# Two attention layers with their gradients on one core: sums of p k v^T over three blocks taken into the first pass, and their K blocks left out of the last

## The chip, the cores and the metric

One core of a Trainium2 chip. A time is the device time of one execution in microseconds (us); the time before is the median of three runs. PE is TensorE's matrix multiply, PEld its weight load, DVE VectorE, ACT ScalarE, POOL GpSimd, SP SyncE, which issues most loads. The arena is a part of SBUF; PSUM is where matmuls put their results.

## The reference

A decode step of four layers with its whole gradient: attention, feed-forward, attention, feed-forward, each after a layer norm and added to x. Both attention layers use the same K and V caches (4 key-value heads, called groups, of 65536 positions and 128 columns, 64 MiB each for K and V in bf16) and the same weights; 8 query heads share a group.

```python
def _A_ref(x, k_cache, v_cache, wq, wo):
    ...
    scores = jnp.einsum("bhqd,bhkd->bhqk", q, k) * (Dh ** -0.5)
    p = _softmax(scores, axis=-1)
    o = jnp.einsum("bhqk,bhkd->bhqd", p, v)
    ...
_out, _vjp = jax.vjp(_f, A_x, A_k_cache, A_v_cache, A_wq, A_wo, B_w1, B_b1, B_w2, B_b2)
_grads = _vjp(grad_out)
```

The outputs are x and the gradients of x, K, V and all weights and biases. The gradient of the query of a layer is, for each head, dq = scale x sum over positions of p (dO v^T - delta) k. Written out, that is dO applied to the 128 x 128 matrix sum of p k v^T, less delta times the vector sum of p k; so a part of the positions can be summed as matrix and vector in a pass in which dO is not yet known, and dq of these positions follows later without K and V.

## The kernel before

Each of the two layers needs p of all positions twice, forward and backward, and K and V do not fit on the chip. So they are read in four passes, p = 0 to 3 in the code (pass 1 to 4 in this text):

- **Pass 1** (`attn_fwd(0, L1, ...)`): forward of layer 1. K is turned by PE (`kT`, L1050) and copied out of PSUM by DVE or ACT (`evac`, L164 and L167), multiplied with the queries (`kS`, L1068), the exponentials are kept for all later passes in a plane of the arena per group (`E`), and V is multiplied with them (`v8`, L1151).
- **Pass 2** (`attn_fwd(1, L3, ...)`): the same for layer 3.
- **Pass 3** (`attn_bwd3(2, L3, ...)`): dq of layer 3: V is turned, multiplied with dO (`vS`), and K with the result (`k8`, L1379).
- **Pass 4** (`attn_bwd4`): dq of layer 1 and the gradients of K and V for both layers, which are stored. K is needed for dq of layer 1 alone (`k8`, L1570); V is turned (L1458) and multiplied with dO of both layers (`vS`, L1495). The outer products of the weights' gradients run in between.

Between the passes lie the dense parts: the last `wo`, the feed-forward layers, and the way back.

**Blocks, units, order.** A block is 4096 positions of one group (32 on each of 128 partitions), 1 MB for K and as much for V; a group has 16 blocks. A step of a pass handles 8 of the 32, so 4 steps make a block and 256 a pass. A unit is 4 blocks (16 steps); the running maximum of the softmax is renewed per unit. `ITEMS[p]` lists the steps of pass p. Before, passes 1 and 2 go group by group (0 to 3 up, then 3 to 0 down), so that the last K blocks of pass 1 stay in the arena for pass 2 (`plan_keep`, 8 K blocks; 7 V blocks each at the next two ends). `pipeline` runs the stages of a step with fixed lags, in that written order on PE, DVE and ACT (`manual_schedule`); pass 4 is not under it, and there the scheduler orders the instructions.

**The arena.** 20 slots of 1 MB: 12, and 8 that become the planes of exponentials of the two layers as the passes reach their groups (`plane`, `hold`). All else, loads of K, V and weights (`slabs`) and outputs, goes through the free slots; SP issues loads in program order, each as soon as its slot is free. In pass 1 two neighbouring free slots are taken at once where they are to be had (`NOW["pairs"]`, `take_pair`, L373: loads of 2 MB); the other passes load 1 MB at a time (L368).

**The sums of pass 2.** Three blocks (`SUMMED`), one of group 3 and two of group 2, are handled in pass 2 by `g_pkv` beside the pipeline: POOL makes the products p k (L1186, 4 heads at a time), PE multiplies V with them (L1179) and sums p k (L1195), one step of the generator per step of the pass, some 66 steps for a block. The results are kept in `PKV`, M (128 x 8 x 128) and S (128 x 8) per group, rescaled by DVE when the maximum has changed. K and V of such a block stay in the arena for as long (`KV["long"]`). Pass 3 then skips K and V of these blocks; `pkv_dq` (L1304, L1305) gives their part of dq from M, S, dO and delta (`nd2`), one call per group within pass 3, and `k8` adds it to the unit's sum.

**Background.** `Background` gives out other work by steps: `by_group` starts the generator of the next group's q (`g_q`) or dO some steps ahead of the group, and `need` runs what is left of it when the group begins. `dO_finish` (L971 to L985) ends each dO: dO itself, the delta product on PE (L976), and its two bf16 halves in `nd2`.

Of the kernel before, what the change touches and what calls it, by code (L numbers as in the profile page):

```python
# [20 lines left out]
def kernel(  # L21
# [251 lines left out]
    HELD, BUSY, RING = set(), set(), set()  # L273
    NOW = {"step": 0, "pairs": True, "wide": False, "newest": False, "ring": False}

# [3 lines left out]
    def plane(lay, g):  # L279

        return NSLOT + G + g if lay else NSLOT + G - 1 - g

# [71 lines left out]
    def kv8(t, g, c8):  # L354
# [3 lines left out]
        if key not in have:  # L358
            i = None
            if NOW["pairs"] and hb % 2 == 0 and (t, g, hb + 1) not in have and key not in KV["halves"]:  # L360
                i = take_pair()
            if i is None:
                at = None
                if key in KV["long"]:
                    at = min((f, i) for i, f in FREE.items() if i < NSLOT)[1]
                    del FREE[at]
                sl = Slot("blk_" + t, at=at, load=True)
                nc.sync.dma_start(out=sl.t.rearrange("p (j d) -> p j d", d=DH), in_=half(KVIN[t], g, hb))  # L368
                have[key] = sl
            else:  # L370
                for h in range(2):
                    have[(t, g, hb + h)] = Slot("blk_" + t, at=i + h)
                nc.sync.dma_start(out=wide(i).rearrange("p (j d) -> p j d", d=DH), in_=KVIN[t][g][hb // 2])  # L373
        return have[key].t.rearrange("p (j d) -> p j d", d=DH)[:, j:j + 8, :]

    def turned_to(t, g, c8, kb8):

        if KV["turn"] == t and (t, g, c8 // J) in KV["keep"] and (t, g, c8 // J) not in MKEYS:
            state_key = (t, g, c8)
# [53 lines left out]
    def start_pass(p):  # L433
# [363 lines left out]
    class Background:  # L797
# [36 lines left out]
        def by_group(self, p, gen):  # L834
# [188 lines left out]
    def attn_fwd(p, L, on_group, bg, end=()):  # L1023
# [116 lines left out]
        def v8(g, c8):  # L1140
# [18 lines left out]
        def g_pkv(g, hb):  # L1159

            ks, vs = (KV["have"][(t, g, hb)] for t in "kv")
            k3, v3 = (sl.t.rearrange("p (j d) -> p j d", d=DH) for sl in (ks, vs))
            M, S = PKV[g]
            before = next((b * J // SU for a, b in SUMMED if a == g and b != hb), None) if (g, hb) != next(m for m in SUMMED if m[0] == g) else None
            if before is None:
# [85 lines left out]
        last_unit = (items[-1][0], items[-1][1] // SU)  # L1251
        n = len(items) // G
        order = list(dict.fromkeys(g for g, _ in items))
        holds = [(k * n + 2, plane(p, g)) for k, g in enumerate(order) if k > 0]
# [25 lines left out]


    def attn_bwd3(p, L, on_group, bg, end=()):
        st = ExitStack()
# [8 lines left out]
        for g, c8 in items:  # L1292
# [3 lines left out]
            hblast[(g, c8 // HB)] = c8  # L1296

        def pkv_dq(g):

            M, S = PKV[g]  # L1300

            pt = ps_mv([P, 2, R])
            for h in range(R):
                nc.tensor.matmul(pt[:, 0, h:h + 1], lhsT=M[:, h, :], rhs=L["dOT"][:, g * R + h:g * R + h + 1], start=True, stop=True)  # L1304
            nc.tensor.matmul(pt[:, 1, :], lhsT=sel2[:, :], rhs=L["nd2"][:, gsl(g)], start=True, stop=True)  # L1305
            t = dspool.tile([P, R], F32, name="pkv_t", tag="pkv_t", bufs=1)
            nc.vector.tensor_tensor(out=t[:], in0=pt[:, 1, :], in1=S[:], op=ALU.mult)
            y = dspool.tile([P, R], F32, name="pkv_y", tag="pkv_y", bufs=1)
            nc.vector.tensor_tensor(out=y[:], in0=pt[:, 0, :], in1=t[:], op=ALU.add)
            state["pkv"] = y  # L1310

# [54 lines left out]
        def k8(g, c8):  # L1366
# [3 lines left out]
            if c8 == sufirst[(g, su)]:  # L1370
                state["ps_dq"] = ps_acc([P, 8, R])
                if SUM_AT.get(g) == su:
                    pkv_dq(g)
            ps_dq = state["ps_dq"]
# [8 lines left out]
            if c8 == sulast[(g, su)]:  # L1383

                def fold():
                    col = ps_dq[:, 0, :]
                    if SUM_AT.get(g) == su:
                        both = dspool.tile([P, R], F32, name="pkv_t", tag="pkv_t", bufs=1)
# [13 lines left out]
    def attn_bwd4(p, La, Lb, on_group, bg, stack, end=()):  # L1402
# [7 lines left out]
        glast = {g: [c8 for gg, c8 in items if gg == g][-1] for g in range(G)}  # L1410
        sufirst, sulast = {}, {}
        for g, c8 in items:
            sufirst.setdefault((g, c8 // SU), c8)
            sulast[(g, c8 // SU)] = c8

# [141 lines left out]

        def k8(g, c8):
            kb8 = kv8("k", g, c8)
            b, j0 = divmod(c8, J)  # L1560
            su = c8 // SU
            X = state[("X", g, b)]
            if c8 == sufirst[(g, su)]:
                state["ps_dq"] = ps_acc([P, 4, R2])
            ps_dq = state["ps_dq"]
            for i in range(8):
# [238 lines left out]
    PKV = {}
    pkv_stack = ExitStack()
    pkv_pool = pkv_stack.enter_context(tc.tile_pool(name="pkv", bufs=1))
    for g in SUM_AT:
        PKV[g] = pkv_pool.tile([P, R, P], F32, name="pkv_m%d" % g), pkv_pool.tile([P, R], F32, name="pkv_s%d" % g)
    attn_fwd(1, L3, on2, bg, [(3, pre_load("wo3", lambda: wo_slabs(lastg[1], 2)))])  # L1810
# [261 lines left out]
    with tc.manual_schedule(engines=ORDERED):  # L2072
# [125 lines left out]
```

## Time and profile before

| | us |
|---|---|
| median of three runs | 1920.0 |
| the three runs | 1920.0, 1918.35, 1925.62 |
| the profiled execution | 1925.24 |
| its span | 1923.5 |

| engine | busy us | share of the span |
|---|---|---|
| PE | 1618.7 | 84% |
| PEld | 1301.0 | 68% |
| DVE | 1194.1 | 62% |
| ACT | 1046.0 | 54% |
| POOL | 340.0 | 18% |

DMA moves 781.38 MB at a mean of 406 GB/s. Of the loads, 60 are of 2048 KB (K 32, V 28, all in pass 1) and 364 of K and V of 1024 KB.

Rows of the profile: a group of instructions has line, engine, operation, out<-in with shapes, x count, then busy us and mean ns of one, then the idle time just before them and what ended it. In the table by stage a row is a window in us from the span's start, with each engine's busy us and instructions, the granted TensorE clock as a share of full speed, the share of time that the DMA engines are busy, and GB/s. In rows of waits, "SPq" is SP's DMA queue: what it waited for, us in total, times, longest.

### The profile page before, as it was taken

Reading aid. Unit: us, or ns where it says so; the run is one execution under the profiler, and the core shown is the slowest. Engines: PE = TensorE matmul, PEld = TensorE weight load, DVE = VectorE, ACT = ScalarE, POOL = GpSimd, SP = SyncE. Lnnn points to the kernel's source line nnn. Section 1 sums busy time; section 2 is a strip of 40 time slices with the busy share of each in tenths; the row PEclk is TensorE's granted clock in tenths of the full one; section 3 lists DMA queues with packets and bytes.
Section 4 is the critical chain, followed back from the end, with each engine's and each line's share of the span. In section 5 each row is a group of like instructions: output and inputs, shape, how many; then the busy total and the mean of one; then the engine's idle time right before and its main releaser. Section 6 shows DMA issues by size and latency. Waiting matters only on the chain. (4 is left out here: it accounts for less than half of the span.)

```text
span 1923.5 us, 67347 instructions
## 1 busy us (share of the span) xinstructions
PE 1618.7 (84%) x30165; PEld 1301.0 (68%) x30165; DVE 1194.1 (62%) x2471; ACT 1046.0 (54%) x1623; POOL 340.0 (18%) x517
## 2 busy tenths in 40 slices
PE   6878788689998987987888888889988979798896
PEld 6878777578887877887777775555555555455463
DVE  5645455266665664555464487767867777567685
ACT  3435343354443445455364376666867777567676
POOL 0000000005776760000000002111111112111121
PEclk9989998899999999999899999888988889789897
DMA  9999999999999999999999997999999999999997
GB/s 393 427 427 424 428 428 416 404 418 422 422 422 418 423 424 333 398 424 422 425 422 423 381 352 300 426 420 396 424 424 423 418 394 413 384 367 424 415 420 327
DMA packets 121489, 781.38 MB, mean 406 GB/s; under 512 B 11104, under 2 KB 18286, under 8 KB 43886
## 3 DMA queue, kind: packets, MB, share of 16 engines
q1 hardware_dynamic: 92894, 602.98, 76.0%
q0 software_dynamic: 24080, 165.70, 20.7%
q10 hardware_dynamic: 4224, 8.39, 1.1%
q8 instruction: 236, 3.87, 0.7%
q14 instruction: 55, 0.45, 0.1%
HBM read 611.33 MB, written 165.69 MB: 404 GB/s over the span
## 5 line engine op out<-in xcount | busy, mean ns | idle before, releaser
L167 DVE COPY kt<-ps_tr 128x1024 bf16<-128x1024 bf16 x728 | 498.9, 687 | 386.3 <-PE ps_tr L1050 217.1
L164 ACT CAST arena<-ps_gg 128x1024 bf16<-128x1024 f32 x457 | 444.4, 1011 | 200.4 <-PE ps_gg L1539 140.8
L1050 PE MATMUL ps_tr<-ident_b,arena 128*128 128x128 bf16 x3840 | 302.1, 222 | 27.6 <-DMA arena<-in_A_k_cache_dram 20.1
L164 ACT COPY kt<-ps_tr 128x1024 bf16<-128x1024 bf16 (+1 forms) x176 | 183.8, 1048 | 194.4 <-PE ps_tr L1320 105.6
L1050 PEld LDWEIGHTS <-arena 128*128 128x128 bf16 x3840 | 238.8, 99 | 55.3 <-DMA arena<-in_A_k_cache_dram 23.2
L167 DVE CAST arena<-ps_gg 128x1024 bf16<-128x1024 f32 (+2 forms) x186 | 222.2, 1195 | 85.1 <-PE ps_gg L1539 48.7
L1151 PE MATMUL ps_acc<-arena 128*128 128x64 bf16 (+4 forms) x4096 | 200.6, 195 | 45.7 <-DMA arena<-in_A_v_cache_dram 36.9
L1539 PE MATMUL ps_gg<-GG,xt 64*128 64x512 bf16 x1024 | 217.2, 421 | 16.5 <-ACT arena L164 5.4
L1186 POOL TENSOR_TENSOR pk<-arena 128x512 bf16<-128x512 bf16 x192 | 195.6, 1042 | 110.7 <-PE ps_m L1179 80.8
L1458 PE MATMUL ps_tr<-ident_b,arena 128*128 128x128 bf16 x1824 | 182.3, 236 | 37.5 <-DVE kt L167 19.3
L1068 PE MATMUL ps_sc<-L_qpad,kt 128*128 128x64 bf16 (+3 forms) x3648 | 183.1, 192 | 16.7 <-issue 8.1
L1133 ACT ACTIVATE arena<-S_sb,L_negm 128x128 bf16<-128x128 f32 x256 | 165.6, 1006 | 53.8 <-DVE L_negm L1118 45.5
L1151 PEld LDWEIGHTS <-arena 128*128 128x128 bf16 x4096 | 156.1, 100 | 50.6 <-DMA arena<-in_A_v_cache_dram 42.3
L1458 PEld LDWEIGHTS <-arena 128*128 128x128 bf16 x1824 | 121.2, 105 | 96.4 <-issue 76.0
L1320 PE MATMUL ps_tr<-ident_b,arena 128*128 128x128 bf16 x1904 | 150.8, 223 | 20.8 <-DMA arena<-in_A_v_cache_dram 19.1
L1068 PEld LDWEIGHTS <-kt 128*128 128x128 bf16 x3648 | 151.8, 99 | 22.3 <-issue 10.5
L661 POOL MEMSET rows_m<- 128x28 f32 (+1 forms) x3 | 0.4, 121 | 818.4 <-DVE rows_ym L754 818.4
L1545 POOL DMA_DIRECT2D out_dram<-arena x128 | 68.5, 535 | 409.6 <-ACT arena L164 263.9
L1570 PEld LDWEIGHTS <-arena 128*128 128x128 bf16 x2048 | 91.6, 102 | 60.7 <-issue 30.9
L1320 PEld LDWEIGHTS <-arena 128*128 128x128 bf16 x1904 | 114.1, 100 | 25.1 <-DMA arena<-in_A_v_cache_dram 21.4
L1133 ACT ACTIVATION_READ_ACCUMULATOR arena<-S_sb,L_negm 128x1 f32 x256 | 128.3, 501 | 0.0
L1495 PEld LDWEIGHTS <-kt 128*128 128x128 bf16 x1824 | 85.8, 102 | 50.4 <-issue 48.8
(359 smaller groups left out, 2475.6 us busy)
## 6 DMA issues: line engine op xcount, KB each, us to landing
arena<-in_A_v_cache_dram SPq DMA_DIRECT2D x183, 1024.0 KB, 16.4
arena<-in_A_k_cache_dram SPq DMA_DIRECT2D x181, 1024.0 KB, 16.7
out_dram<-arena POOLq DMA_DIRECT2D x149, 1024.0 KB, 15.3
arena<-in_A_k_cache_dram SPq DMA_DIRECT2D x32, 2048.0 KB, 28.5
arena<-in_A_v_cache_dram SPq DMA_DIRECT2D x28, 2048.0 KB, 29.9
arena<-in_A_wo_dram SPq DMA_DIRECT2D x30, 1024.0 KB, 17.0
arena<-in_B_w_dram SPq DMA_DIRECT2D x21, 1024.0 KB, 11.1
arena<-in_A_wq_dram SPq DMA_DIRECT2D x20, 1024.0 KB, 13.7
```

The lines of the kernel that those rows point to most:

```text
L164: nc.scalar.copy(out=out, in_=in_)
L167: nc.vector.tensor_copy(out=out, in_=in_)
L1050: nc.tensor.transpose(pt[:, i, :], kb8[:, i, :], ident_b[:, :])
L1068: nc.tensor.matmul(state["ps_s"][:, s:s + w, :].rearrange("p a b -> p (a b)"), lhsT=kt[:, i, :], rhs=L["qpad"][:, g, 0:w, :].rearrange("p ...
L1133: nc.scalar.activation(out=E(p, g, c0, SU)[:, :, h], in_=S[:, h, :], func=ACTF.Exp, bias=L["negm"][:, g, su, h:h + 1], scale=SCALE, accum_ ...
L1151: NOW["ps_o"] = nc.tensor.matmul(ps_o[:, 0:w, :], lhsT=vb8[:, i, :], rhs=E(p, g, c, w), start=(c % SU == 0), stop=(c % SU == SU - 1), skip ...
L1186: nc.gpsimd.tensor_tensor(out=r[:, :, :], in0=k3[:, j, :].unsqueeze(1).to_broadcast([P, 4, P]), in1=e4.unsqueeze(2).to_broadcast([P, 4, P] ...
L1320: nc.tensor.transpose(pt[:, i, :], vb8[:, i, :], ident_b[:, :])
L1458: nc.tensor.transpose(pt[:, i, :], vb8[:, i, :], ident_b[:, :])
L1495: nc.tensor.matmul(state["ps_dp"][:, s:s + w, :].rearrange("p a b -> p (a b)"), lhsT=vt[:, i, :], rhs=DOB[:, g, 0:w, :].rearrange("p a b - ...
L1539: nc.tensor.matmul(pg[:, 512 * h:512 * h + 512], lhsT=xt[64 * h:64 * h + 64, j1 // 8 + m, :], rhs=gg[64 * h:64 * h + 64, :, :].rearrange(" ...
L1570: nc.tensor.matmul(ps_dq[:, 0:w, :].rearrange("p a b -> p (a b)"), lhsT=kb8[:, i, :], rhs=X[:, s:s + w, :].rearrange("p a b -> p (a b)"), ...
```

## The change

- Pass 1 now also runs `g_pkv`, over blocks 0, 4 and 7 of group 3, for layer 1. M and S are opened ahead of pass 1 and closed ahead of pass 4.
- `pkv_dq` is called for layer 1 at the end of the dense part between pass 3 and pass 4, after dO of group 3; `k8` of pass 4 skips the three K blocks (their V is still loaded) and adds the result in unit 1 of group 3.
- The blocks summed in pass 2 are now blocks 8, 7 and 0 of group 3, all in one M and S; pass 3 skips three K and V pairs as before.
- The units of passes 1 and 2 come in an order written out: group 3's come between those of others. The planes, the holds and the starts of `by_group` follow that order.
- Loads of two slots at once are off in pass 1 (`NOW["pairs"]`).

```diff
-    NOW = {"step": 0, "pairs": True, "wide": False, "newest": False, "ring": False}
+    NOW = {"step": 0, "pairs": False, "wide": False, "newest": False, "ring": False}
...
-        return NSLOT + G + g if lay else NSLOT + G - 1 - g
+        return NSLOT + G + g if lay else NSLOT + G - 1 - list(dict.fromkeys(g for g, _ in ITEMS[0])).index(g)
...
-    ITEMS = [order_by_unit(False, SU), order_by_unit(True, SU), order_by_unit(False, HB), order_by_unit(True, J)]
+    def units(p, order):
+        assert sorted(order) == [(g, u) for g in range(G) for u in range(NSU)]
+        return [(g, c8) for g, u in order for c8 in range(u * SU, (u + 1) * SU, 8)]
+
+    ORDER1 = [(0, 0), (3, 0), (0, 1), (0, 2), (0, 3), (3, 1), (1, 0), (1, 1), (1, 2), (1, 3), (2, 0), (2, 1), (2, 2), (2, 3), (3, 2), (3, 3)]
+    ORDER2 = [(3, 3), (3, 2), (3, 1), (2, 3), (2, 2), (2, 1), (2, 0), (1, 3), (1, 2), (3, 0), (1, 1), (1, 0), (0, 3), (0, 2), (0, 1), (0, 0)]
+    ITEMS = [units(0, ORDER1), units(1, ORDER2), order_by_unit(False, HB), order_by_unit(True, J)]
     MG, MB = ITEMS[1][0][0], ITEMS[1][0][1] // J - 4
-    SUMMED = [(MG, MB), (MG - 1, MB), (MG - 1, 3)]
-    SUM_AT = {g: hb * J // SU for g, hb in SUMMED}
-    ITEMS[2] = [(g, c8) for g, c8 in ITEMS[2] if (g, c8 // J) not in SUMMED]
-    MKEYS = [(t,) + m for m in SUMMED for t in "kv"]
+    SUMS = [[(MG, 0), (MG, 4), (MG, 7)], [(MG, MB), (MG, 7), (MG, 0)]]
+    SUM_AT = [s[-1][1] * J // SU for s in SUMS]
+    ITEMS[2] = [(g, c8) for g, c8 in ITEMS[2] if (g, c8 // J) not in SUMS[1]]
+    MKEYS = [[(t,) + m for m in s for t in "kv"] for s in SUMS]
...
-        NOW["pairs"] = p == 0
+        NOW["pairs"] = False
         KV["halves"] = set(TOUCH[p][-8:])
-        KV["long"] = set(MKEYS if p == 1 else [])
+        KV["long"] = set(MKEYS[p] if p < 2 else [])
...
-                self.later.append((k * n + 8 if PS["pass4"] and k else k * n + n // (2 if p in (1, 2) and k == 0 else 4), gen(g), g))
+                first = next(i for i, (gg, _) in enumerate(ITEMS[p]) if gg == g) if p < 2 else (k + 1) * n
+                self.later.append((max(4, first - (n - 8 if PS["pass4"] and k else n // 2 if p in (1, 2) and k == 0 else 3 * n // 4)), gen(g), g))
...
-            if p == 1 and c8 % J == 0 and (g, c8 // J) in SUMMED:
+            if c8 % J == 0 and (g, c8 // J) in SUMS[p]:
                 sides.append(g_pkv(g, c8 // J))
...
-        PS["m"] = p == 1
+        PS["m"] = True
...
+    def pkv_dq(lay, L, pool):
+
+        M, S = PKV[lay]
+        pt = ps_mv([P, 2, R])
+        for h in range(R):
+            nc.tensor.matmul(pt[:, 0, h:h + 1], lhsT=M[:, h, :], rhs=L["dOT"][:, MG * R + h:MG * R + h + 1], start=True, stop=True)
+        nc.tensor.matmul(pt[:, 1, :], lhsT=sel2[:, :], rhs=L["nd2"][:, gsl(MG)], start=True, stop=True)
+        t = pool.tile([P, R], F32, name="pkv_t", tag="pkv_t", bufs=1)
+        nc.vector.tensor_tensor(out=t[:], in0=pt[:, 1, :], in1=S[:], op=ALU.mult)
+        y = vec.tile([P, R], F32, name="pkv_y%d" % lay)
+        nc.vector.tensor_tensor(out=y[:], in0=pt[:, 0, :], in1=t[:], op=ALU.add)
+        return y
...
         def k8(g, c8):
+            if (g, c8) == items[len(items) // G - 1]:
+                first_at(1, lambda: state["Xs"].free())
+            if (g, c8 // J) in SUMS[0]:
+                return
             kb8 = kv8("k", g, c8)
...
-                fold_dq(La, g, su, ps_dq[:, 0, 0:R], gfirst[g] // SU == su, glast[g] // SU == su, dspool)
+                col = ps_dq[:, 0, 0:R]
+                if (g, su) == (MG, SUM_AT[0]):
+                    both = dspool.tile([P, R], F32, name="pkv_both", tag="pkv_both", bufs=1)
+                    nc.vector.tensor_tensor(out=both[:], in0=col, in1=PKV["y"][:], op=ALU.add)
+                    col = both[:]
+                fold_dq(La, g, su, col, gfirst[g] // SU == su, glast[g] // SU == su, dspool)
...
         while rows.queue:
             rows.back()
         next(wo_it, None)
+        PKV["y"] = pkv_dq(0, L1, DENSE["pool"])
     dst.close()
+    PKV_STACK[0].close()
     psA_stack.close()
```

More of the change, by code (lines that the diff above doesn't have):

```diff
@@ L359, in kv8 @@
             i = None
-            if NOW["pairs"] and hb % 2 == 0 and (t, g, hb + 1) not in have and key not in KV["halves"]:
+            if (NOW["pairs"] and hb % 2 == 0 and (t, g, hb + 1) not in have and key not in KV["halves"]
+                    and not {key, (t, g, hb + 1)} & KV["long"]):
                 i = take_pair()
@@ L376, in turned_to @@
     def turned_to(t, g, c8, kb8):
-        if KV["turn"] == t and (t, g, c8 // J) in KV["keep"] and (t, g, c8 // J) not in MKEYS:
+        if KV["turn"] == t and (t, g, c8 // J) in KV["keep"] and (t, g, c8 // J) not in MKEYS[1]:
             state_key = (t, g, c8)
@@ L1162, in g_pkv @@
             k3, v3 = (sl.t.rearrange("p (j d) -> p j d", d=DH) for sl in (ks, vs))
-            M, S = PKV[g]
-            before = next((b * J // SU for a, b in SUMMED if a == g and b != hb), None) if (g, hb) != next(m for m in SUMMED if m[0] == g) else None
+            M, S = PKV[p]
+            n = SUMS[p].index((g, hb))
+            before = SUMS[p][n - 1][1] * J // SU if n else None
             if before is None:
@@ L1251, in attn_fwd @@
         last_unit = (items[-1][0], items[-1][1] // SU)
-        n = len(items) // G
         order = list(dict.fromkeys(g for g, _ in items))
-        holds = [(k * n + 2, plane(p, g)) for k, g in enumerate(order) if k > 0]
+        holds = [(next(i for i, (gg, _) in enumerate(items) if gg == g) + 2, plane(p, g)) for g in order[1:]]
         if p == 0:
@@ L1296, in attn_bwd3 @@
             hblast[(g, c8 // HB)] = c8
[L1298 to L1310, printed above, removed]
         def vT(g, c8):
@@ L1371, in k8 @@
                 state["ps_dq"] = ps_acc([P, 8, R])
-                if SUM_AT.get(g) == su:
-                    pkv_dq(g)
+                if (g, su) == (MG, SUM_AT[1]):
+                    state["pkv"] = pkv_dq(1, L, dspool)
             ps_dq = state["ps_dq"]
@@ L1386, in fold @@
                     col = ps_dq[:, 0, :]
-                    if SUM_AT.get(g) == su:
+                    if (g, su) == (MG, SUM_AT[1]):
                         both = dspool.tile([P, R], F32, name="pkv_t", tag="pkv_t", bufs=1)
@@ L1411, in attn_bwd4 @@
         sufirst, sulast = {}, {}
+        kfirst = {}
         for g, c8 in items:
             sufirst.setdefault((g, c8 // SU), c8)
-            sulast[(g, c8 // SU)] = c8
+            if (g, c8 // J) not in SUMS[0]:
+                kfirst.setdefault((g, c8 // SU), c8)
+                sulast[(g, c8 // SU)] = c8
         def g_setup(g):
@@ L1562, in k8 @@
             X = state[("X", g, b)]
-            if c8 == sufirst[(g, su)]:
+            if c8 == kfirst[(g, su)]:
                 state["ps_dq"] = ps_acc([P, 4, R2])
@@ L1571, in k8 @@
                                  rhs=X[:, s:s + w, :].rearrange("p a b -> p (a b)"),
-                                 start=(c == sufirst[(g, su)]), stop=(c == sulast[(g, su)] + 7), skip_group_check=True)
+                                 start=(c == kfirst[(g, su)]), stop=(c == sulast[(g, su)] + 7), skip_group_check=True)
             kv_done("k", g, c8)
-            if (g, c8) == items[len(items) // G - 1]:
-                state["Xs"].free()
             if c8 == sulast[(g, su)]:
-                fold_dq(La, g, su, ps_dq[:, 0, 0:R], gfirst[g] // SU == su, glast[g] // SU == su, dspool)
+                col = ps_dq[:, 0, 0:R]
[4 more added lines that the diff above has]
+                fold_dq(La, g, su, col, gfirst[g] // SU == su, glast[g] // SU == su, dspool)
                 if glast[g] // SU == su:
@@ L1725, in g_w2, with pkv_open @@
         yield from g_mv(w2_slabs()[0], FC, DC, lambda kc: L["gb"][:, kc:kc + 1], ps, fin, side=side)
+    PKV, PKV_STACK = {}, {}
+    def pkv_open(lay):
+        PKV_STACK[lay] = ExitStack()
+        pool = PKV_STACK[lay].enter_context(tc.tile_pool(name="pkv%d" % lay, bufs=1))
+        PKV[lay] = pool.tile([P, R, P], F32, name="pkv_m%d" % lay), pool.tile([P, R], F32, name="pkv_s%d" % lay)
+    pkv_open(0)
     hold(plane(0, ITEMS[0][0][0]))
@@ L1804, in on2 @@
             bg.add(g_wo(L3, x3, g))
[L1805 to L1809, printed above, removed]
+    pkv_open(1)
     attn_fwd(1, L3, on2, bg, [(3, pre_load("wo3", lambda: wo_slabs(lastg[1], 2)))])
@@ L1991 @@
     bg.drain()
-    pkv_stack.close()
+    PKV_STACK[1].close()
     reset_load()
```

## The prediction

> **What bounds the kernel now.** I read the page first (its 40 slices), then a table by stage, then the waits of PE and of SP's DMA queue in single stages, then single lines. "Pass 1" to "pass 4" are the four sweeps over K and V, p = 0 to 3 in the code.
>
> ```profile
> DMA  9999999999999999999999997999999999999997
> GB/s 393 427 427 424 428 428 416 404 418 422 422 422 418 423 424 333 398 424 422 425 422 423 381 352 300 426 420 396 424 424 423 418 394 413 384 367 424 415 420 327
> ```
>
> The DMA engines are busy in every slice but one and the end; only the places between passes (slices 8, 16 and 17, 23 to 25) and some of pass 4 fall under 410 GB/s. The limit is bytes over a rate, so I need the rate of each stage, and which engine is next behind it. The stages (columns: window, its length, PE, PEld, DVE, ACT, POOL busy, granted clock, DMA share, GB/s) are pass 1, pass 2 with its sums on POOL, pass 3, the change from pass 3 to 4, two stretches of pass 4, and one slow place in it:
>
> ```profile
> 65.00:320.00 255.00, 204.44 (x4827) 194.70 (x4824) 138.87 (x318) 106.27 (x261) 0.00 (x0) 0.95 1.01 427
> 438.00:718.00 280.00, 257.64 (x5688) 226.52 (x5685) 177.52 (x367) 122.62 (x295) 195.59 (x192) 1.00 1.01 422
> 820.00:1060.00 240.00, 197.77 (x4370) 181.98 (x4366) 127.60 (x258) 119.88 (x170) 0.00 (x0) 0.95 1.01 423
> 1140.00:1190.00 50.00, 41.26 (x708) 30.00 (x706) 35.19 (x90) 30.25 (x36) 8.25 (x17) 0.93 0.79 295
> 1200.00:1280.00 80.00, 66.88 (x832) 42.33 (x831) 59.29 (x105) 54.87 (x67) 14.24 (x28) 0.87 1.01 425
> 1330.00:1520.00 190.00, 166.57 (x2057) 104.83 (x2054) 140.24 (x254) 139.03 (x167) 34.24 (x64) 0.88 1.01 424
> 1655.00:1700.00 45.00, 34.34 (x287) 19.31 (x286) 22.39 (x35) 21.93 (x26) 4.29 (x8) 0.51 0.86 332
> ```
>
> Two things are to be seen. Pass 1, the only pass that loads 2 MB at a time, runs at 427 GB/s; everything with 1 MB loads runs at 422 to 425. And pass 2 already carries exactly the work that pass 1 is to get (POOL products, PE sums): PE is 92% busy there (257.64 of 280) and DMA does not suffer beyond what pass 3 shows without sums.
>
> **The change, part by part.** The profiled execution took 1925.24 us (span 1923.5, 1.7 around it); the median of the three runs is 1920.0, so the profile is one of the slow ones by 5.2 us. I sum differences against it and apply them to the median.
>
> *K blocks skipped in pass 4.* Three loads of 1 MB, 3 x 1.0486 = 3.15 MB (the built program issues 242 K blocks' worth instead of 245, so this does happen). At 424 GB/s that is 7.4 us; bounds are 0, if another limit holds there, and 9.5, at the 332 GB/s of the slow place. The blocks 7, 4 and 0 of group 3 lie in the stretch 1200 to 1340, of which the table shows 425 at a full DMA share. Can PE follow? In that stretch:
>
> ```profile
> PE ps_acc L1570 <- DMA arena<-in_A_k_cache_dram: 6.2, 2, 4.5
> PE ps_tr L1458 <- DMA arena<-in_A_v_cache_dram: 2.6, 1, 2.6
> ```
>
> PE waits 8.8 us for loads, and it also loses 96 matmuls of L1570 (23.7 us busy for 397, so 5.7 us): 14.5 us of room for 7.4. I take -7.4.
>
> *2 MB loads become 1 MB loads in pass 1.* 60 loads, 125.8 MB. At 427 they take 294.6 us; at 423 (pass 3, 1 MB loads, no POOL) 297.4; at 422 298.1; at 424 296.7. That is +2.1 to +3.5; I take +2.8, as pass 3 is the row with the same traffic and nothing else. SP issues 60 more instructions of about 0.33 us; in pass 3 it does so at 423.
>
> *The sums in pass 1.* 192 products on POOL and 192 matmuls on PE, each summed block 64 and 64, beside 96 small matmuls of p k:
>
> ```profile
> L1186 POOL TENSOR_TENSOR pk<-arena 128x512 bf16<-128x512 bf16 x192 | 195.6, 1042 | 110.7 <-PE ps_m L1179 80.8
> ```
>
> and, from that line's own list (shortest, median, longest in ns),
>
> ```profile
> L1179 PE MATMUL ps_m<-pk,arena x192: 376/380/390, 451.7 to 717.7; 128*128 128x512 bf16 x192
> ```
>
> POOL has 195.6 us of new work in a pass where it is idle. PE gets 192 x 0.38 = 73 us by these spans, which overlap others. I cost it at nothing: the cover is PE's idle time, 50 us in 255 of pass 1, and pass 2 shows the same load on PE at 422 GB/s. Without the cover it costs what PE runs over; that is the slow rival.
>
> The blocks to be summed stay in the arena over some 70 steps each, so fewer slots are free. In pass 2, which holds as many, the last thing that SP waits for is, for 65 us of 280, the landing of an earlier load and not a slot:
>
> ```profile
> SPq L368 <- PE ps_tr L1050: 124.8, 52, 6.2
> SPq L368 <- DMA arena<-in_A_k_cache_dram: 35.6, 25, 3.0
> SPq L368 <- DMA arena<-in_A_v_cache_dram: 25.6, 23, 2.4
> SPq L472 <- DMA arena<-in_A_k_cache_dram: 4.1, 2, 2.1
> ```
>
> and pass 1 holds fewer planes of exponentials than pass 2. Nothing for that.
>
> *`pkv_dq` for layer 1, between pass 3 and 4.* In before, two such calls lie in pass 3 (16 fp32 matmuls and one of `sel2` each). The new one stands on PE between the delta product of `dO_finish` (L976) and the first matmuls of pass 4 (L1495), both in the timeline below, after one of the old calls:
>
> ```profile
> 1073.61 1.93 PE L1304 MATMUL ps_mv<-L_dOT,pkv_m 128*128 128x1 f32 x16
> ...
> 1075.47 0.18 PE L1305 MATMUL ps_mv<-L_nd,sel 64*128 64x8 bf16 x1
> ...
> 1156.96 0.23 PE L976 MATMUL ps_mv<-dlt_prod,ones_f 128*33 128x8 f32 x2 [0.46 <-DVE dlt_prod L973]
> 1157.43 0.74 PE L1495 MATMUL ps_sc<-DOB,arena 128*128 128x64 bf16 x20 [0.25 <-DVE negd L979]
> ```
>
> So L1495 starts 1.93 + 0.18 = 2.1 us later. Queued behind it on PE is all of pass 4's start, and SP stands still for exactly these matmuls: between 1140 and 1190 it waits 14.9 and 12.9 us for L1495, at 295 GB/s. Nothing hides it. Bounds: 0, and 4.1 (the other call in before took 3.55 at half clock, 0.18, and two DVE steps of 0.17). I take +2.1. Pass 3 has one call fewer; there DMA is the limit, so that gives 0 (bound -2.1).
>
> *The interleaving.* q of group 3 is now due at step 16, and its weights are loaded from step 4 on. The pass starts with an empty arena, and SP's queue runs ahead to the tenth or so load by 10 us, so I cost it at 0; the bound is one landing, 13.7 us (the page's median for `wq`), if PE had to wait for the second slab. Planes are held 16 steps earlier in pass 2: 0, by the free slots above. About 30 small DVE instructions (0.17 us) more: 0, DVE is 63% busy in pass 2.
>
> Sum: -7.4 + 2.8 + 2.1 = -2.5 us; 1922.7 for an execution like the profiled one, 1917.5 on the median.
>
> **A rule against it.** DVE's small operations on two SBUF operands do slow down beside POOL: `df` (L1121) takes 167 ns in pass 1 and 586 in pass 2, while the PSUM copies of K (L167) take 691 and 689. The Trainium skill says so too (SBUF — State Buffer, "Who interferes with whom": a VectorE instruction with two SBUF inputs and a GpSimd instruction that reads SBUF exclude each other for the whole instruction); the trace agrees, and by it every such operation of pass 1 may come to wait up to the length of a POOL product, and the sum would grow as in the fourth rival. What it costs here is a rival below, from rows.
>
> **The rivals.**
>
> *Pass 1 turns PE-bound (slower).* In pass 1 the granted clock is 0.95, so 0.05 x 255 = 12.8 us of PE's time are lost to windows at half clock. Today this is free, as PE is idle for 50 us. With the sums PE is 92% busy, and if the windows stay and fall where PE has no room, pass 1 grows by them: -2.5 + 12.8 = +10.3, 1930.3. It decides as soon as the lost time exceeds PE's waits for loads, which are 12.3 us in the 280 of pass 2 (9.8 at L1151, 2.5 at L1050). For it: little room. Against it: in pass 2, with the sums, the clock was 1.00 from 438 to 718. The Trainium skill (TensorE: Matmul & The Clock Gate, "Part 1: The HAM clock gate") says that activity of PE is what releases its throttle; by that rule the sums take the windows away, and pass 2 agrees. 0.13.
>
> *The saving is not had.* Pass 4 has PE 84 to 88% and DVE and ACT 69 to 74% busy, and SP there waits mostly for PE to free slots. If the loop of slots is the limit and not the rate, the three loads leave and nothing moves: +2.8 + 2.1 = +4.9, 1924.9. Against: a DMA share of 1.01 wherever the blocks lie. 0.14.
>
> *A slow window of pass 4 goes away (faster).* Pass 4's instructions are put in order anew by the scheduler. Between 1655 and 1700 the clock is 0.51 and DMA moves 332 instead of 424: 45 x (1 - 332/424) = 9.8 us lost. If another order does not fall into this, -2.5 - 9.8 = -12.3, 1907.7. Against: the causes lie in short gaps of PE, which the new order will have too, elsewhere. 0.12.
>
> *VectorE becomes late in pass 1.* It is 63% busy in pass 2 and 54% in pass 1; if all of that went on the path it would be 0.09 x 280 = 25 us, but PE waited for DVE only 2.5 us there (1.3 at L1068, 1.2 at L955). Price 2.5: 1920.0. 0.05.
>
> **How the numbers follow.** 0.56 stays for the forecast, 1917.5; its own range from the bounds is 1914 to 1922. A measurement of this kernel tells about 0.5%, 9.6 us, from no change. Faster by more: the slow window's case and a trace of the forecast's tail, 0.13. Slower by more: most of the PE-bound case and little of the others, 0.13. Within: 0.74. The range 1908 to 1929 leaves out about half of the one outer case, most of the other and some tails, 0.18 in all.
>
> **What would show it.** In the profile after: the first eight slices at 421 to 424 GB/s instead of 427; POOL busy in them; a clock near 1.00 in pass 1; PE there at about 92% with some waits for loads left (none left would be the PE-bound case); 3.1 MB less in the DMA total; `pkv_dq` ahead of pass 4's first matmuls, with L1495's successor about 2 us later after the last `dO`; group 3 of pass 4 shorter by about 7 us. Wrong would be: pass 1 under 420 GB/s over more than a slice, PE without waits for loads in it, or a group 3 of pass 4 as long as before.

## The result, and the profile after

The changed kernel takes 1951.43 us (median of six runs, 1946.04 to 1954.91) against 1919.17 us before; the ratio is 1.0158, 95% interval 1.0132 to 1.0184. It is 30 us slower, where 2.5 us less was forecast and 1929 was the upper end of the range. The profiled execution took 1946.04 us, its span is 1944.3. The ratios are not quotients of the medians and can differ from them by a thousandth or two; where that matters both are given.

The slices of the page after, with POOL's row above them (40 slices of 48.6 us, busy tenths, then GB/s):

```profile
POOL 0377767004776660000000001111111211122211
...
DMA  9999999999999999999999997999999999899998
GB/s 382 414 417 416 417 418 412 385 411 414 418 414 417 412 417 335 386 416 416 418 415 415 397 344 269 425 419 388 352 424 425 424 420 422 337 396 423 424 421 336
```

POOL works in pass 1 now. The DMA engines are about as busy as before. But wherever passes 1 to 3 run at their full rate, that rate is 411 to 418 GB/s; it was 427 in pass 1 and 422 to 425 in the others. From slice 26 on, in pass 4, the full rate is 424 to 425 as before. The stages (window, length, PE, PEld, DVE, ACT, POOL, granted clock, DMA share, GB/s):

```profile
65.00:320.00 255.00, 232.81 (x5096) 205.11 (x5097) 162.59 (x336) 105.88 (x257) 176.19 (x174) 0.99 1.01 417
438.00:718.00 280.00, 255.42 (x5574) 225.64 (x5575) 176.47 (x372) 120.07 (x290) 185.83 (x183) 0.99 1.01 415
840.00:1080.00 240.00, 194.07 (x4273) 178.67 (x4270) 122.15 (x247) 112.28 (x156) 0.00 (x0) 0.95 1.02 416
1160.00:1210.00 50.00, 40.02 (x698) 30.16 (x696) 33.56 (x88) 28.53 (x35) 6.37 (x13) 0.97 0.73 273
1220.00:1300.00 80.00, 67.42 (x819) 41.62 (x818) 59.95 (x109) 55.27 (x67) 14.19 (x27) 0.85 1.01 422
1330.00:1400.00 70.00, 61.32 (x603) 33.80 (x599) 48.93 (x88) 51.78 (x61) 11.53 (x23) 0.73 0.95 364
1420.00:1600.00 180.00, 155.69 (x2037) 98.19 (x2037) 134.45 (x244) 129.70 (x155) 31.77 (x62) 0.89 1.01 424
1675.00:1720.00 45.00, 31.29 (x345) 18.10 (x344) 29.36 (x44) 28.39 (x34) 7.86 (x14) 0.77 0.81 306
```

The first three rows have a DMA share of 1.01 or 1.02 at 415 to 417 GB/s: the same busy time moves fewer bytes. Pass 3 shows it too, which has no sums and, but for the three blocks that it skips, the old order. The sixth row is a slow stretch that the kernel before does not have: clock 0.73, 364 GB/s. The last one is the slow place that it does have.

Two times along the way say where the 20.8 us between the two profiled executions lie: the end of pass 2 is 15.4 us later (741.1 to 756.5) and the start of pass 4 24.0 us later (1159.0 to 1183.0, first `X`); pass 4 itself is only 3.2 us shorter (764.5 to 761.3). The profile before was one of the long executions and this one is the shortest of its six, so the difference of the medians, 32.3 us, is some 11 us larger than these show.

### The profile page after: what moved, and what is told of

Read it like the earlier page. It is cut to its first block, busy times and chain, and to the rows that moved or that the text cites. A ratio compares the mean times of both kernels' runs of the same rounds, so it can differ in the third digit from the quotient of the medians.

```text
span 1944.3 us, 68129 instructions
## 1 busy us (share of the span) xinstructions
PE 1646.5 (85%) x30357; PEld 1309.5 (67%) x30357; DVE 1225.2 (63%) x2515; ACT 1047.5 (54%) x1624; POOL 536.4 (28%) x709
## 3 DMA queue, kind: packets, MB, share of 16 engines
q0 software_dynamic: 24080, 165.70, 20.5%
## 5 line engine op out<-in xcount | busy, mean ns | idle before, releaser
L164 ACT CAST arena<-ps_gg 128x1024 bf16<-128x1024 f32 x456 | 445.6, 1015 | 178.3 <-PE ps_gg L1549 108.3
L1195 POOL TENSOR_TENSOR pk<-arena 128x512 bf16<-128x512 bf16 x384 | 391.2, 1042 | 259.1 <-PE ps_m L1188 164.2
L1058 PE MATMUL ps_tr<-ident_b,arena 128*128 128x128 bf16 x3840 | 297.4, 220 | 10.4 <-issue 7.0
L164 ACT COPY kt<-ps_tr 128x1024 bf16<-128x1024 bf16 (+1 forms) x176 | 184.6, 1052 | 222.6 <-PE ps_tr L1327 125.2
L1058 PEld LDWEIGHTS <-arena 128*128 128x128 bf16 x3840 | 247.8, 98 | 57.8 <-issue 13.2
L1549 PE MATMUL ps_gg<-GG,xt 64*128 64x512 bf16 x1024 | 214.7, 418 | 45.4 <-DVE arena L167 27.1
L1159 PE MATMUL ps_acc<-arena 128*128 128x64 bf16 (+4 forms) x4096 | 206.8, 196 | 40.4 <-DMA arena<-in_A_v_cache_dram 30.2
L1468 PE MATMUL ps_tr<-ident_b,arena 128*128 128x128 bf16 x1824 | 178.0, 233 | 19.2 <-DVE T L1452 8.9
L1159 PEld LDWEIGHTS <-arena 128*128 128x128 bf16 x4096 | 159.9, 101 | 46.8 <-DMA arena<-in_A_v_cache_dram 34.5
L1327 PE MATMUL ps_tr<-ident_b,arena 128*128 128x128 bf16 x1904 | 151.7, 224 | 21.8 <-DMA arena<-in_A_v_cache_dram 19.8
L1468 PEld LDWEIGHTS <-arena 128*128 128x128 bf16 x1824 | 117.7, 103 | 74.9 <-issue 63.4
L1076 PEld LDWEIGHTS <-kt 128*128 128x128 bf16 x3648 | 150.8, 98 | 22.0 <-ACT kt L164 11.6
L1188 PE MATMUL ps_m<-pk,arena 128*128 128x512 bf16 x384 | 144.5, 381 | 0.6 <-DVE pkv_m L1211 0.3
L1327 PEld LDWEIGHTS <-arena 128*128 128x128 bf16 x1904 | 114.8, 100 | 26.3 <-DMA arena<-in_A_v_cache_dram 22.1
L1549 PEld LDWEIGHTS <-xt 64*128 64x128 bf16 x1024 | 63.7, 94 | 95.6 <-issue 60.3
## 6 DMA issues: line engine op xcount, KB each, us to landing
arena<-in_A_wq_dram SPq DMA_DIRECT2D x24, 1024.0 KB, 18.5
```

The source lines that it names most:

```text
L164: nc.scalar.copy(out=out, in_=in_)
L1058: nc.tensor.transpose(pt[:, i, :], kb8[:, i, :], ident_b[:, :])
L1076: nc.tensor.matmul(state["ps_s"][:, s:s + w, :].rearrange("p a b -> p (a b)"), lhsT=kt[:, i, :], rhs=L["qpad"][:, g, 0:w, :].rearrange("p ...
L1159: NOW["ps_o"] = nc.tensor.matmul(ps_o[:, 0:w, :], lhsT=vb8[:, i, :], rhs=E(p, g, c, w), start=(c % SU == 0), stop=(c % SU == SU - 1), skip ...
L1188: nc.tensor.matmul(acc[:, :, :].rearrange("p a b -> p (a b)"), lhsT=v3[:, j, :], rhs=r[:, :, :].rearrange("p a b -> p (a b)"), start=j == ...
L1195: nc.gpsimd.tensor_tensor(out=r[:, :, :], in0=k3[:, j, :].unsqueeze(1).to_broadcast([P, 4, P]), in1=e4.unsqueeze(2).to_broadcast([P, 4, P] ...
```

## The experiments

In each, the diff is against the kernel named. Four kernels and the kernel before shared a chip; before had medians of 1920.8 (e1 to e4), 1921.9 (e5 to e8) and 1921.1 us (e9 to e12).

**What could slow passes 1, 2 and 3 alike?** Among the edits there is one that no step of the prediction looked at: the result of `pkv_dq` is a tile of 32 bytes per partition from `vec`, one for each layer. The arena is allocated behind `vec`, so it starts 64 bytes higher: at byte 47936 of each partition instead of 47872, which is 187 x 256. The small pools between `vec` and the arena (`tmp`, `ktpool`, `mvs`) move with it.

**e1: the changed kernel with the arena back in its place.**

```diff
-        y = vec.tile([P, R], F32, name="pkv_y%d" % lay)
+        y = x0 if lay else x1
```

> The changed kernel with one edit: the two results of pkv_dq are written into tiles that are dead by then, so that no new tile is allocated and the arena starts again where it does in the kernel before, at byte 47872 of each partition (a multiple of 256) and not at 47936 (64 over one). Theory of the moved arena: passes 1 to 3 go from 417, 415 and 416 GB/s back to about 423, and with some 1050 us in passes 1 to 3 this is 1.4% of them, 13 to 15 us: about 1936. Rival (the sums or the interleaving slow the loads): 416 GB/s stays and the time stays at about 1951. What is left over 1919 then belongs to the 1 MB loads, to pkv_dq and to pass 4.

Measured: 1932.66 us, ratio to before 1.0056 (1.0036 to 1.0076). The stages of passes 1, 2 and 3:

```profile
65.00:320.00 255.00, 236.93 (x5136) 208.45 (x5134) 163.98 (x341) 108.82 (x267) 179.09 (x176) 0.98 1.01 423
438.00:718.00 280.00, 257.29 (x5706) 227.49 (x5704) 180.05 (x377) 120.62 (x292) 193.70 (x191) 1.00 1.01 423
840.00:1060.00 220.00, 177.93 (x3961) 162.65 (x3957) 112.66 (x224) 102.95 (x141) 0.00 (x0) 0.97 1.01 423
```

417, 415 and 416 GB/s have become 423 in all three, with the sums, the order and everything else left in. That takes off 1.0158 - 1.0056 = 0.0102, or 19.6 us; I had expected 13 to 15. In the traces pass 4 begins 16.6 us earlier (first `X` at 1183.0, then at 1166.4).

**e2: the kernel before with the arena moved, nothing else.**

```diff
+    pad = vec.tile([P, 16], F32, name="pad")
+    nc.vector.memset(pad[:], 0.0)
```

> The kernel before with an unused tile of 64 bytes per partition allocated ahead of the arena, and nothing else; it is cleared once by VectorE. The arena then starts at byte 47936. Theory of the moved arena: 8 KB packets of the loads go from 309 to 312-319 ns, passes 2 and 3 from 422 and 423 to 415-417 GB/s, pass 1 with its 2 MB loads a little less than 427 too; 13 to 15 us more, about 1933. Rival (the place of the arena means nothing): 422 to 427 GB/s and 1919.

Measured: 1939.66 us, ratio 1.0101 (1.0072 to 1.0131), 19.4 us. Passes 1, 2, 3, and a stretch of pass 4:

```profile
65.00:320.00 255.00, 203.26 (x4777) 193.96 (x4774) 137.74 (x316) 103.34 (x251) 0.00 (x0) 0.94 1.01 423
438.00:718.00 280.00, 256.28 (x5647) 226.18 (x5642) 175.34 (x365) 121.44 (x291) 189.21 (x186) 0.99 1.01 413
820.00:1060.00 240.00, 198.37 (x4350) 182.37 (x4346) 127.26 (x255) 116.80 (x165) 0.00 (x0) 0.94 1.02 416
1220.00:1290.00 70.00, 59.37 (x732) 37.18 (x733) 53.42 (x97) 47.10 (x57) 12.78 (x25) 0.85 1.01 425
```

An unused tile of 64 bytes costs as much as e1 gained. Even the 2 MB loads of pass 1 fall from 427 to 423, but pass 4 does not fall: it begins 14.8 us later than in before (1159.0, then 1173.8) and is no longer. In the trace's records of single packets, those of 8 KB take a median of 309 ns in passes 1 to 3 of before and of e1, and 312 ns in the changed kernel and in e2 (means 309 to 312 against 315 to 317). The pools that moved along are no target of these loads, so their longer packets point to the arena; no run moves the arena alone.

**e8 and e12: which places are good?** As e2 with a tile of 256 bytes, and of 128.

> As e2, but the unused tile has 256 bytes per partition: the arena starts at 48128, a multiple of 256 as in the kernel before (47872). If it is the place modulo 256 that counts: 8 KB packets at 309 ns, 422 to 427 GB/s, 1920 as before. If any other place is slower, or if the added tile itself is what slows the loads: about 1939 as in e2. If 512 counts (48128 is a multiple of it, 47872 is not): faster than before.

> As e2 and e8, with 128 bytes: the arena starts at 48000, a multiple of 128 but not of 256. If the place modulo 256 counts and any remainder is equally bad: 1939, as with 64. If it is graded: between 1920 and 1939. If 128 is enough: 1920.

Measured: with 256 bytes 1922.34 us, ratio 0.9988 (0.9964 to 1.0011), no difference; with 128 bytes 1934.12 us, ratio 1.0079 (1.0051 to 1.0108). Pass 2 with 256 bytes, then with 128:

```profile
438.00:718.00 280.00, 259.45 (x5740) 228.56 (x5738) 179.75 (x369) 124.69 (x302) 195.58 (x192) 1.00 1.01 423
```

```profile
438.00:718.00 280.00, 253.67 (x5607) 223.62 (x5606) 174.73 (x362) 121.70 (x291) 189.20 (x186) 1.00 1.01 416
```

In these four places it is the remainder modulo 256 bytes that counts, not the added tile; a multiple of 512 is no better, and 128 over a multiple is about as bad as 64 over (the intervals overlap). The Trainium skill (DMA: Bandwidth & Descriptors, "How a descriptor splits into AXI transactions") says that a transaction must start at a multiple of 256 B, and that the first one of a descriptor that does not start there begins at the multiple below, where the unused bytes still cost beats of 32 B. It says so of reads, with examples below 1 KB. If it held for the writes here, an 8 KB row 64 bytes over would need two beats more on 256, an estimate of 0.8%, and one 128 bytes over four, an estimate of 1.6%. The packets here became 1.0% longer by their medians at 64 and at 128 bytes alike (309 to 312 ns), and 1.2 to 1.7% by their means in passes 2 and 3. So the trace agrees with the page in kind; the size does not grow with the offset as the beats would, and the mechanism is not shown.

**e3: 1 MB loads in pass 1.** The kernel before with `NOW["pairs"]` off.

```diff
-    NOW = {"step": 0, "pairs": True, "wide": False, "newest": False, "ring": False}
+    NOW = {"step": 0, "pairs": False, "wide": False, "newest": False, "ring": False}
...
-        NOW["pairs"] = p == 0
+        NOW["pairs"] = False
```

> The kernel before with 1 MB loads in pass 1 too, and nothing else. The prediction's term: pass 1 at 422 to 424 GB/s instead of 427, +2.8 us (2.1 to 3.5), about 1922. If 1 MB loads are worse in pass 1 than in pass 3, pass 1 would fall to about 417 and the time would be about 1926.

Measured: 1923.15 us, ratio 1.0025 (1.0009 to 1.0042), 4.8 us (1.7 to 8.1), 2.3 by the medians; pass 1 at 423 GB/s, the value taken in the prediction:

```profile
65.00:320.00 255.00, 204.41 (x4847) 194.68 (x4843) 139.01 (x318) 109.26 (x263) 0.00 (x0) 0.96 1.01 423
```

In the traces the end of pass 2 moves from 741.1 to 744.5, 3.4 us. In e1, with the sums and the new order on top, it is 744.7. So both together cost 0.2 us in the two passes: the prediction's nought stands.

**e4: the 2 MB loads back into the changed kernel** (e1 with `NOW["pairs"] = p == 0`).

> As e1, and pass 1 loads 2 MB at a time again where the blocks are not to be summed. If the term of the 2 MB loads adds up with that of the arena: 2 to 3 us less than e1, about 1933, pass 1 at 425 to 427 GB/s. If pairs need more free slots than the held blocks of the sums leave, no gain, pass 1 at 423 or less.

Measured: 1948.69 us, ratio 1.0163 (1.0125 to 1.0202), slower than e1 by 16.0 us in the medians and 20.5 in the ratios: one of its four runs took 1960.31 us, and the trace is of that one. Pass 1 in it:

```profile
65.00:320.00 255.00, 234.31 (x5122) 206.04 (x5119) 163.66 (x338) 107.86 (x261) 177.79 (x176) 0.99 0.99 416
```

What SP waited for last in pass 1, in e4 and then in e1 (L374 issues loads of 2 MB, L369 of 1 MB):

```profile
SPq L374 <- PE ps_tr L1058: 99.3, 18, 10.7
SPq L374 <- PE ps_acc L1159: 54.8, 8, 10.4
SPq L374 <- PE ps_m L1188: 47.7, 9, 11.6
```

```profile
SPq L369 <- DMA arena<-in_A_k_cache_dram: 90.3, 44, 3.5
SPq L369 <- DMA arena<-in_A_v_cache_dram: 83.0, 41, 3.6
```

With pairs SP waits for slots that PE still reads, the sums' matmuls (L1188) among them; with single slots the last thing is the landing of an earlier load. So the held blocks seem to leave too few pairs of free slots: turning the pairs off belongs to the sums, at its price of e3.

**The slow stretch of pass 4.** In the changed kernel, SP's waits from 1330 to 1400, and PE in it:

```profile
SPq L369 <- PE ps_tr L1468: 55.7, 4, 20.2
```

```profile
1365.49 0.61 PE L1549 MATMUL ps_gg<-GG,xt 64*128 64x512 bf16 x2 [0.51 <-ACT arena L164]
1366.41 0.61 PE L1549 MATMUL ps_gg<-GG,xt 64*128 64x512 bf16 x2 [0.30 <-ACT arena L164]
1367.32 0.61 PE L1549 MATMUL ps_gg<-GG,xt 64*128 64x512 bf16 x2 [0.31 <-ACT arena L164]
1368.33 0.61 PE L1549 MATMUL ps_gg<-GG,xt 64*128 64x512 bf16 x2 [0.40 <-DVE arena L167]
...
1377.70 0.61 PE L1549 MATMUL ps_gg<-GG,xt 64*128 64x512 bf16 x2 [0.40 <-DVE arena L167]
1378.45 0.61 PE L1483 MATMUL ps_tr<-ident_b,xin 128*128 128x128 bf16 x4
1378.86 1.38 PE L1468 MATMUL ps_tr<-ident_b,arena 128*128 128x128 bf16 x11
```

From 1364 to 1378 PE makes nothing but outer products, each pair waiting for ACT or DVE to copy the one before it out of PSUM. The turns of V (L1468), which free the slots that SP waits for, stand behind them. In the order of the program this is a run of 32 such matmuls (26 of L1549 and 6 of L1634; 8 of them make an output of 1 MB); in the order of before no run is longer than 4 until the last 1% of the program. So the scheduler of pass 4 put them together. DVE's product `X` points to the reason: in the changed kernel, in e7 (below) and in before, the line of its extra semaphore events:

```profile
L1526 DVEq EVENT_SEMAPHORE  x10: 21/21/203, 1183.0 to 1726.4; - x10
```

```profile
L1516 DVEq EVENT_SEMAPHORE  x13: 21/21/275, 1158.5 to 1693.3; - x13
```

```profile
L1516 DVEq EVENT_SEMAPHORE  x1: 21/21/21, 1159.0 to 1159.0; - x1
```

`X` now also waits for copies into the arena; the trace shows a wait for ACT's (L164). It reads the exponentials of both layers in one strided view, `bass.ds(plane(0, g), 2, step=plane(1, g) - plane(0, g))`. Before, the planes of a group are nested: slots 12 and 19 for group 3, 13 and 18 for group 2. The change gives layer 1's planes out in the order in which its groups begin, so group 3 has 14 and 19, group 2 has 12 and 18. When group 3 is done, slot 14 takes an output, and it lies between group 2's two planes, and between group 1's (13 and 17). Group 0 has 15 and 16 with nothing between them. That fits the line: the last extra event, at 1726.4, is in group 1, and group 0 has none.

**e5: e1 with the planes nested again.**

```diff
-        return NSLOT + G + g if lay else NSLOT + G - 1 - list(dict.fromkeys(g for g, _ in ITEMS[0])).index(g)
+        return NSLOT + G + g if lay else NSLOT + G - 1 - g
```

> As e1, and the planes of layer 1 lie again in the slots of the kernel before: plane(0, g) = NSLOT + 3 - g, so that the planes of the two layers are nested (12 and 19 for group 3, 13 and 18 for group 2, and so on). With the changed order of planes group 3's plane is slot 14, which lies between group 2's planes 12 and 18; pass 4 reads two planes in one strided view. Theory of the planes: in e1 the product X of group 2 waits until an output that was put into slot 14 is complete (32 outer-product matmuls in a row, PE 1347 to 1364 us, loads at about 350 GB/s for 70 us, some 13 us lost). Here that place goes back to 424 GB/s, and the time to about 1920. Rival (the three absent K loads make PE the limit of pass 4 there, with the clock at 0.75): the slow stretch stays, 1932. The wait for a wq slab of 18.5 us near 1656 us in e1 is a thing of its own: if it goes too, about 1910.

Measured: 1924.05 us, ratio 1.0006 (0.9988 to 1.0024), 0.0050 or 9.6 us below e1. The stretch of 70 us that begins 160 us into pass 4, in e1 and then in e5:

```profile
1326.00:1396.00 70.00, 61.50 (x632) 35.04 (x631) 49.75 (x86) 53.71 (x66) 12.06 (x24) 0.75 0.91 347
```

```profile
1321.00:1391.00 70.00, 63.03 (x765) 39.47 (x764) 55.14 (x98) 54.55 (x68) 12.72 (x25) 0.89 1.01 406
```

The run of outer products is gone and 406 GB/s are back (not 424), 765 matmuls instead of 632. `X` is back to one extra event:

```profile
L1526 DVEq EVENT_SEMAPHORE  x1: 21/21/21, 1161.4 to 1161.4; - x1
```

The wait for wq did not go (17.3 us in this trace). The runs spread from 1913 to 1927, and the trace is of the shortest.

**e7: the kernel before with the changed planes, nothing else.**

```diff
-        return NSLOT + G + g if lay else NSLOT + G - 1 - g
+        return NSLOT + G + g if lay else NSLOT + G - 1 - [0, 2, 3, 1][g]
```

> The kernel before with the planes of layer 1 in the changed kernel's slots (groups 0, 1, 2, 3 in slots 15, 13, 12, 14), and nothing else. Theory of the planes: pass 4 gets the run of outer products ahead of group 2's second product, some 13 us, about 1933, with DVE's X waiting for ACT's or DVE's copies into the arena. Rival (the stretch comes from the skipped K blocks): no change, 1920.

Measured: 1927.62 us, ratio 1.0039 (1.0019 to 1.0058), 7.5 us (5.7 by the medians). A run of outer products comes with the planes alone, 22 matmuls at 1341 to 1352 us; `X` has its extra events (above), and one kind of wait that before does not have:

```profile
DVE X L1516 <- ACT arena L164: 0.9, 2, 0.5
```

K is loaded in full here, so the run does not come from the skipped blocks. But its price in loads does in part. Summed up in windows of 10 us, what is lost against 425 GB/s from 130 to 230 us of pass 4 is 16.0 us in e1 (run, and blocks skipped), 6.1 in e5 (blocks skipped, no run), 4.9 in e7 (run, K loaded) and 4.0 in before: only both together are dear. Most of the 7.5 us of e7 must lie elsewhere in the new order of pass 4 and are not located. That the planes cause the run is shown, and that they cost time, from both sides; that it is the slot between the two ends of the view is read from the waits and the slots' numbers.

**e6: e5 with the three K blocks back.**

```diff
         def k8(g, c8):
...
-            if (g, c8 // J) in SUMS[0]:
-                return
...
-                if (g, su) == (MG, SUM_AT[0]):
+                if False:
```

> As e5, but pass 4 loads the K of the three blocks again and multiplies it, and the result of pkv_dq is not added (the sums of pass 1 are made and not used). This is the prediction's term of -7.4 us the other way round: by the theory that the saving is had where the loads are the limit, e6 is 7 to 8 us above e5. Rival (the loop of slots is the limit of that stretch): e6 equals e5.

Measured: 1929.46 us, ratio 1.0050 (1.0031 to 1.0069), above e5 by 0.0044 or 8.4 us in the ratios (some 3 to 13 with both intervals) and by 5.4 us in the medians. The three blocks cost time, and about as much as forecast (7.4). Where they cost it is another matter. The 100 us that begin 130 us into pass 4, in e5, in e6 and in before:

```profile
1291.00:1391.00 100.00, 90.84 (x1067) 56.09 (x1065) 77.29 (x144) 75.03 (x89) 17.63 (x34) 0.86 1.00 400
```

```profile
1293.00:1393.00 100.00, 90.75 (x1123) 57.04 (x1123) 77.94 (x146) 76.78 (x92) 18.83 (x36) 0.90 1.01 422
```

```profile
1289.00:1389.00 100.00, 92.88 (x1116) 57.75 (x1115) 78.03 (x145) 75.57 (x90) 18.82 (x36) 0.86 1.00 408
```

Without the three blocks the loads fall to 400 GB/s here, with them they run at 422: 2.2 MB of the 3.1 that were skipped, some 5 us of the 7.4, are lost again here, about where the last of the three lies and behind it. SP waits 74.6 us for the turns of V there in e5, and 38.2 in e6. Against before, at 408, it is 0.8 MB or 2 us. Up to 213 us into pass 4 both kernels keep the same pace (the 21st product `X` starts there in each); the last `X` starts at 702 us in e5 and at 718 in e6. So most of the difference arises later, where both load the same blocks in another order, and that the missing bytes alone make it is not shown.

**e10: e5 without `pkv_dq` of layer 1.**

```diff
-                if (g, su) == (MG, SUM_AT[0]):
+                if False:
...
-        PKV["y"] = pkv_dq(0, L1, DENSE["pool"])
```

> As e5 without the call of pkv_dq for layer 1 and without the addition of its result: the three blocks' part of dq is left out. The prediction's term: 2.1 us less than e5, 1922, with PE's first matmul on dO in pass 4 at the same distance from the dense part as in the kernel before (28.6 to 30.3 us after the last x4 matmul, 32 to 35 with the call). If pkv_dq costs what these distances say, 3 to 4 us: 1920.

This kernel leaves out the three blocks' part of dq. Measured: 1919.85 us, ratio 0.9991 (0.9967 to 1.0014), 0.0015 or 2.9 us below e5, with overlapping intervals. The traces are clearer. PE from the delta product to pass 4's first matmuls in e5, then in e10:

```profile
1156.03 0.23 PE L984 MATMUL ps_mv<-dlt_prod,ones_f 128*33 128x8 f32 x2 [0.46 <-DVE dlt_prod L981]
1156.51 1.95 PE L1295 MATMUL ps_mv<-L_dOT,pkv_m 128*128 128x1 f32 x16 [0.25 <-DVE negd L987]
1158.39 0.18 PE L1296 MATMUL ps_mv<-L_nd,sel 64*128 64x8 bf16 x1
1159.03 0.66 PE L1505 MATMUL ps_sc<-DOB,arena 128*128 128x64 bf16 x9 [0.46 <-DVE x L1300]
```

```profile
1155.77 0.23 PE L984 MATMUL ps_mv<-dlt_prod,ones_f 128*33 128x8 f32 x2 [0.46 <-DVE dlt_prod L981]
1156.25 1.07 PE L1505 MATMUL ps_sc<-DOB,arena 128*128 128x64 bf16 x32 [0.25 <-DVE negd L987]
```

L1505 starts 3.00 us after L984 with the call and 0.48 without: 2.5 us, the 16 + 1 matmuls of the forecast and 0.46 more, in which PE waits for DVE to finish `y`.

**e9 and e11: a longer lead for the wq slabs.** In several of the kernels DVE waits in pass 4 for a slab of wq, with PE and ACT behind it (18.5 us in the changed kernel, 17.3 in e5). Both kernels ask 12 steps ahead instead of 8.

```diff
-        steps = 8 if PS["pass4"] else WAIT_STEPS
+        steps = 12 if PS["pass4"] else WAIT_STEPS
```

> As e5, and in pass 4 the products that read a new slab of wq or wo come 12 steps after its load is asked for instead of 8 (a step is 3 us, and the load of wq near 1656 us took 24.6 us to land in e1). In e5 DVE waits 17.3 us for that slab, with PE and ACT behind it, and about 5 us of loads are lost. If that wait goes: 1915 to 1919, below both kernels. If the new order of pass 4 has another place of that kind: 1924 as e5, or more.

> The kernel before with the 12 steps of e9 and nothing else. If the wait for wq (its slow place, 1655 to 1700 us at 332 GB/s) is what costs there, 1912 to 1916; if the new order has such a place elsewhere, 1920 as before. With e9 it tells whether the change is worth anything once that place is gone: by the prediction's sum e9 is 2.5 us below e11, by the measured terms (+4.8 for the 1 MB loads, +3.7 for pkv_dq, -8 for the K blocks) about equal.

Measured: e9 1929.12 us, ratio 1.0042 (1.0027 to 1.0058); e11 1942.79 us, ratio 1.0113 (1.0084 to 1.0141). Both are worse than what they started from. The waits in pass 4, e9 and then e11:

```profile
DVE mv_t L616 <- DMA arena<-in_A_wq_dram: 14.3, 1, 14.3
```

```profile
DVE mv_t L609 <- DMA arena<-in_A_wq_dram: 35.7, 2, 18.3
```

The waits do not go: in e9 it is another slab's, 629 us into pass 4 instead of 492, and e11 has two. More steps between a load and its product, as they are counted when the program is written, do not take them away. What would, I have not found; the cause of these waits stays open, and no version here beats the kernel before. These two runs also say how far a time can be trusted: one number in pass 4 moved it by 7 and by 22 us, as the scheduler orders that pass anew each time. A difference of a few us between kernels with different passes 4 (e5, e6, e7) is therefore not the price of one line unless a trace shows it in its place.

## Why the prediction was wrong

The time was wrong by 34 us (1951.43 against 1917.5), for two side effects that were not in the sum. Term by term, in ratios to before times 1920 us:

| term | predicted | measured | by |
|---|---|---|---|
| arena 64 bytes off (not in the sum) | none | +19.6 | change to e1; +19.4 in e2 |
| order of the planes (in "interleaving") | 0 | +9.6 | e1 to e5; +7.5 in e7 |
| K blocks skipped | -7.4 | -8.4; -5.4 by medians | e6 to e5 |
| 1 MB loads in pass 1 | +2.8 | +4.8 (1.7 to 8.1) | e3 |
| `pkv_dq` | +2.1 | +2.9; 2.5 in the traces at L1505 | e5 to e10 |
| sums and order in passes 1 and 2 | 0 | +0.2 | e1 against e3, end of pass 2 |
| all without the first two | -2.5 | +1.2 (-2.3 to +4.6) | e5 |

The first two rows and the last make 30.4 us, the whole difference (0.0158 x 1920 = 30.3), as they must: the changed kernel, e1, e5 and before are one chain.

*The steps that held.* The table's last row is the prediction's own sum, and its -2.5 lies 0.2 us outside the measured interval: the terms were right in kind, the 1 MB loads and `pkv_dq` perhaps a little too cheap. POOL's work stayed beside the loads, and PE's idle time covered the new matmuls: 91% busy in pass 1, clock 0.99, and PE still waits for loads there (4.5 us). So the PE-bound rival failed, and for the reason that was given against it. The rule of the Trainium skill on VectorE and GpSimd (SBUF — State Buffer, "Who interferes with whom") did come true: the subtraction `df` of pass 1 went from 167 to 839 ns. It cost nothing that shows: 10 such instructions in 255 us, and the end of pass 2 in e1 is where it is in e3.

*The step that failed first* is one that was not made. The change part by part listed what the new instructions cost and not what the new tiles move. Its term is missing, and so it stood at nothing: 64 bytes in front of the arena, measured at +19.6 us. A sign that the prediction had named came up at once: "pass 1 under 420 GB/s over more than a slice". But no rival there had a cause for it other than a PE-bound pass; that pass 3 fell equally, with no sums in it, pointed to the addresses.

*The step that failed second* is "the interleaving: 0". Of the planes it asked only when they are held, not which slots they take. What follows from the slots shows only in pass 4, and there it gave away the saving that the change was made of: 9.6 us against 8.4.

*A step that came out in size and not for its reason* is "I take -7.4". It counts on a full rate for the stretch from 1200 to 1340, and the row that it reads ends at 1280. The rest of that stretch in before:

```profile
1280.00:1340.00 60.00, 52.39 (x606) 32.02 (x606) 42.02 (x86) 38.53 (x43) 10.47 (x21) 0.83 0.98 397
```

With the blocks skipped the loads got slower about the last of them and behind it (400 GB/s in e5, 408 in before, 422 in e6), and what brought the total back lies later in pass 4. That the sum of both is near 7.4 is partly luck.

*The rivals.* "The saving is not had" came nearest, as pass 4 got 3.2 us shorter instead of 7.4. It does not hold as a whole, since e6 is slower than e5; but in that stretch e5 gives much of the saving back while SP waits for PE to free slots, as this rival has it. "A slow window goes away" did not happen: DVE's wait for wq at that place is 18.5 us. The range was too narrow because every rival was about the time of instructions, and none about the places of data.

## What to carry to other kernels

When a change allocates anything, even 32 bytes, compare the addresses of all buffers allocated after it: here a load target 64 or 128 bytes over a multiple of 256 per partition took 1.4 to 2.1% off the rate of passes with 8 KB packets, and no busy row shows it except GB/s at a full DMA share. When a change gives out slots in another order, look at every view that spans several of them; the slots between its ends may become dependences of its readers. And when all stages get slower by the same share, look for what they have in common before looking at what was added to one of them.

## What the runs showed of the hardware

- The loss from an arena that is 64 or 128 bytes off shows only in passes that load and store nothing: 423 to 413-417 GB/s there. In pass 4, where loads and stores of as much data run together, the full rate stayed at 422 to 425, as before. The 8 KB packets there take a median of 309 ns in the changed kernel and in e2, too. Why not there, is open.
- Loads of 2 MB (16 KB packets) suffer less from it: pass 1 falls by 0.9% (427 to 423), passes 2 and 3 by 1.4 to 2.1% (422 to 413-416, 423 to 416-417).
